# Banded attention into a gated two-layer block on one core: weights requested early, one output stage moved ahead of the second batch's attention

## The chip, the cores and the metric

The kernel runs on one core of a Trainium2 chip. The metric is device time in microseconds (us), from three runs: 324.64, 325.49 and 327.11, median 325.49. The core's engines have one instruction queue each: TensorE (PE, matmuls; its weight loads are PEld), VectorE (DVE), ScalarE (ACT), GpSimd (POOL) and SyncE (SP, which here only issues DMAs). An instruction waits for its semaphores at the head of its queue, and all behind it wait with it.

## The reference

Attention in a causal window of 128 positions with a linear bias per head (ALiBi), for 8 batches of 8 heads, 576 positions and 64 values per head; its output, as 4608 tokens by 512, goes through a two-layer block whose gate is h·sigmoid(beta·h).

```python
scores = scale * np.matmul(q, k.transpose(0, 1, 3, 2))
...
bias = slopes[:, None, None] * (-np.abs(rel).astype(np.float32))[None, :, :]
mask = (rel >= 0) & (rel < window)      # window = 128
scores = np.where(mask, scores + bias[None], -1000000000.0)
scores = scores - np.max(scores, axis=-1, keepdims=True)
attn = np.exp(scores)
attn = attn / (np.sum(attn, axis=-1, keepdims=True) + 1e-09)
return np.matmul(attn, v).astype(np.float32)
...
h = x @ w_in                      # x: (4608, 512), w_in: (512, 2048)
g = h * (1.0 / (1.0 + np.exp(-beta * h)))
return (g @ w_out).astype(np.float32)
```

## The kernel before

**Tiling.** The two-layer block works on nine groups g of 512 tokens. H(g) is 16 steps j: four matmuls of 128x512 (L557) make a 128x512 block of h in one PSUM bank, ACT takes its tanh into `sig` (L564), DVE makes (sig + 1)·h into `gT` (L565), which frees the bank. (h·sigmoid is written with tanh, a factor 0.5 comes at the end.) O(g, i, n), for four row blocks i and four parts n, is four matmuls (L588) that add gT times a quarter of w_out into one bank; after part 3 ACT copies the bank out (L598). A *chunk* below is four such matmuls, of H or of O. Weights W1 (four chunks of columns) and W2 (four chunks of rows) are requested by POOL, cast to bf16 on the way.

**Attention.** Rows of q, k, v are requested by SP (L207, L218), at most 14 staging tiles at once, cast to bf16 by POOL. For batches 0 and 1, a head pair p is transposed on PE (`TP`, L287; copied to SBUF by DVE and ACT), and visited twice: visit A has its scores in the two-bank PSUM tile SS, visit B in the two-bank tile SX (`SP_`). ACT takes the exponential; `PVP` multiplies by v and DVE normalises; `XP` transposes the result into XT, which H reads. The bias and the mask come in one of two ways: a matmul with a table (`slope` times `relb`, L324) that adds them to the scores, or a DVE multiplication of the exponentials by exp(bias) (`factor`, from the table `fallq`). The last 64 positions of a batch go their own way (TT, SCT, PV, X). From batch 2 on, DMA transposes take the place of PE ones, scores are `SC`, in SS and in ST, and `PVB` multiplies by v. H(1) needs the tail of batch 0 and the first 448 positions of batch 1.

**Order.** PE, SP and POOL run in the order that the kernel is written in; for batch 0 that holds for ACT and DVE too, after it their order is a scheduler's. The list `steps` sets what PE does between batch 0 and H(1): the H chunks of group 0 with the attention of batch 1 between them. `spread` then runs H(1), O(0) and O(1, 0 to 2), and lays the attention of batch 2 between the items from number `first` on. `b2` holds the requests, casts and DMA transposes of batch 2, one popped with each item.

**PSUM.** Eight banks: SS (2), `hps` (2), transposes (2, later ST), SX (2, later the banks `ops` and `h3`). H blocks take turns: in group 0 steps j = 0 and 3 lie in the halves of SX, the rest in `hps`; in group 1 odd steps below `FOUR[1]` lie in `h3` and `ops`.

Of the kernel before, what the change touches and what calls it, by code (L numbers as in the profile page):

```python
# [10 lines left out]
ALU = mybir.AluOpType  # L11
# [4 lines left out]
P = 128  # L16
# [3 lines left out]
def kernel(  # L20
# [142 lines left out]
    def falls_late(i):  # L163
        to, a, w = ((0, 0, P), (128, 0, 64), (192, 0, P), (320, 1, 64), (384, 1, P))[i]
        after(nc.vector.tensor_copy(
            out=falls[:, :, to : to + w], in_=fall[:, :, a, 0:w]), gates[1, 4])

    def factor(pt, m, p):

        if m:  # L170
            nc.vector.tensor_tensor(  # L171
                out=pt[:], in0=pt[:], in1=falls[:, 2 * p : 2 * p + 2], op=ALU.mult)
            return
        t = (fallq if m is None else fall)[:, 2 * p]
# [138 lines left out]
    def SP_(b, vis, p):  # L313
        qk = QK[b % 2]
        sps = SX if vis == "B" else SS
        w = WIDTH[vis]
        biased = vis == "A" or p > 1
        if biased:
            rhs = relb[:]
            if vis == "B":  # L320
                rhs = bass.AP(tensor=rhs.tensor, offset=rhs.offset,
                              ap=[list(rhs.ap[0]), [2 * P, 2], [0, 2], [1, P]])
            for e in range(2):
                nc.tensor.matmul(  # L324
                    sps[:, e, 0:w], lhsT=slope[:, 2 * p + e], rhs=rhs, start=True, stop=False,
                    skip_group_check=True)
# [13 lines left out]
        pt = pt_pool.tile([P, 2, 512], BF16, name="pt", tag="pt")  # L340
        pts[b, vis, p] = pt
        nc.scalar.activation(out=pt[:, :, 0:w], in_=sps[:, :, 0:w], func=ACTF.Exp, scale=qscale)
        if vis == "B" and b and not biased:
            factor(pt, None, p)

    def room(b, shape):

# [61 lines left out]
    def DT(b, sb):  # L409
        rows = ROWS[sb]  # L410
        src = staged.pop((b, sb))
        moved.add((b, sb))
        r = nc.sync.dma_start(
            out=QK[b % 2][:, :, :, P * sb : P * sb + rows].rearrange("d i p s -> d (i p) s"),
            in_=src[0:rows].rearrange("r i h d -> r (i h d)"), transpose=True,
        )
        if (b, sb) == (2, 0):
            after(r, w2[3])

    COLS = {0: (0, 384), 1: (128, 256), 2: (0, 384), 3: (192, 320), 4: (128, None)}  # L420

# [115 lines left out]


    gts, hs = {}, {}
    FOUR = {1: 10, 2: 8}  # L540

    def Hm(g, j, cs):
        if j == 0 and cs[0] == 0:
            gts[g] = gt_pool.tile([P, NFF, TOKG], BF16, name="gT", tag="gT")
        c0 = (g * TOKG) % XTR
        if cs[0] == 0:
            if g == 0 and j in (0, 3):
                hs[g, j] = SX[:, j // 2]
            elif j % 2 and j < FOUR.get(g, 0):
                hs[g, j] = obank("hpo", "h3" if j % 4 == 1 else "ops")  # L550
            elif g > 1 and j % 3 == 2 and j >= FOUR.get(g, 0):
                hs[g, j] = obank("hpo", "h3")
            else:
                hs[g, j] = psum_h.tile([P, TOKG], F32, name="hps", tag="hps")[:]
        hps = hs[g, j]
        for c in cs:
            nc.tensor.matmul(  # L557
                hps, lhsT=W1[:, c, bass.ts(j, P)], rhs=XT[:, c, c0 : c0 + TOKG],
                start=(c == 0), stop=(c == NDM - 1),
            )  # L560
        if cs[-1] < NDM - 1:
            return
        sig = sig_pool.tile([P, TOKG], BF16, name="sig", tag="sig")
        gates[g, j] = nc.scalar.activation(out=sig[:], in_=hps, func=ACTF.Tanh, scale=beta_h[:, j : j + 1])  # L564
        gates["gT"] = nc.vector.scalar_tensor_tensor(  # L565
            out=gts[g][:, j, :], in0=sig[:], scalar=1.0, in1=hps, op0=ALU.add, op1=ALU.mult
        )
# [6 lines left out]
    def OS(g, i, n):  # L574
        gT = gts[g]
        if n == 0:
            if g < 2:
                late[g, i] = obank("ops", "h3" if i % 2 and (g, i) != (1, 3) else "ops")
            elif i == 0 or i == 2 and g == NTG - 1:
                late[g, i] = psum_h.tile([P, DM], F32, name="oph", tag="hps")[:]  # L580
            else:
                late[g, i] = obank("ops", "ops")
# [89 lines left out]
    with tc.manual_schedule(engines={ENG.PE, ENG.SP, ENG.Pool}):  # L672
        with tc.manual_schedule(engines={ENG.Activation, ENG.DVE}):
# [22 lines left out]
            SP_(0, "A", 1)  # L696
            cast_v(0, 0)
            cast_pair(0, 2)
            w1.append(load_w1(0))
            TP(0, 2)  # L700
            M(0)
            SP_(0, "B", 1)
            cast_v(0, 1)
            idle(2)
            SP_(0, "A", 2)
            PVP(0, "A", 0)
# [4 lines left out]
            PVP(0, "A", 1)  # L711
            cast_v(0, 2)
            cast_v(0, 3)
            w1.append(load_w1(1))
            padding()
            PVP(0, "A", 2)
            SP_(0, "A", 3)
# [41 lines left out]
            cast_qk(b, 4)  # L759
            cast_v(b, 4)  # L760

        for w in ("p0", "p1", "v0", "v1", "p2", "p3", "v2", "v3"):
            n = int(w[1])
            if w[0] == "p":
                get_pair(1, n)
            else:
                get("v", 1, n)
        tail(0)
        tail(1)
        w1.append(load_w1(2))  # L770
        cast_pair(1, 0)
        cast_pair(1, 1)
        cast_v(1, 0)
        cast_v(1, 1)
        cast_pair(1, 2)
        cast_pair(1, 3)
        w1.append(load_w1(3))
        cast_v(1, 2)
        cast_v(1, 3)
        w2 += [load_w2(n) for n in range(2)]  # L780
        tail_casts(0)
        w2 += [load_w2(n) for n in range(2, 4)]
        tail_casts(1)
        OG = lambda g, i: [lambda n=n: OS(g, i, n) for n in range(4)]
        HG = lambda g: [lambda j=j: HS(g, j) for j in range(NFF)]
# [14 lines left out]
                    at += att[done][2]  # L800
                    done += 1

        b2 = blocks(2)

        def wrap(it):
            def f():
                if b2:
# [16 lines left out]
        half = lambda c: lambda: Hm(0, 15, range(c, c + 2))  # L824
        def open_s():
            trans.close()
            psum_s = ctx.enter_context(
                tc.tile_pool(name="psum_s", bufs=1, space=bass.MemoryType.PSUM))
            spans.append(psum_s.tile([P, 2, 512], F32, name="ST"))

        steps = [h[2], R(0), h[3], h[4], A(0), R(1), B_(0), h[5], A(1), h[6], R(2), B_(1), VA(0), falls_tail,
                 h[7], A(2), R(3), h[8], VA(1), B_(2), VB(0), h[9], A(3), VB(1), VA(2), h[10],
                 B_(3), open_o, lambda: TT(0), h[11], VA(3), XO(0), lambda: SCT(0), h[12], VB(2),
                 XO(1), h[13], lambda: PV(0, 4, 0), VB(3), lambda: PV(0, 4, 1), XO(2), h[14],
                 half(0), XO(3), lambda: X(0, 4), half(2)]
        for f in steps:
# [4 lines left out]
        rest = {0: [lambda: TT(1)], 2: [lambda: SCT(1)],  # L841
                4: [lambda: PV(1, 4, 0), lambda: PV(1, 4, 1)], 5: [lambda: X(1, 4), open_s]}
        items = h[:10]
        for n in range(6):
            items += [h[10 + n], o[n]] + rest.get(n, [])
        items += o[6:]
        for n in range(5):
            items.insert(18 + n, lambda n=n: falls_late(n))
# [46 lines left out]
```

The softmax here doesn't subtract the row's maximum and nothing guards it: scores larger than these inputs give would overflow.

## Time and profile before

| | |
|---|---|
| times of three runs | 324.64, 325.49, 327.11 us |
| profiled execution: span, first to last instruction | 324.0 us |
| its own time | not listed apart; the median of the runs is 1.5 us above the span |
| PE busy | 312.7 us, 97% |
| ACT, DVE, POOL busy | 60%, 57%, 30% |
| PE clock granted | full in all 40 slices, mean 0.999 |
| H(0) chunk j = 2, H(1) first chunk, H(2) first chunk on PE | start at 22.35, 49.01 and 94.23 us |

A busy PE counts the tail of each pipelined matmul, so back-to-back chunks are better read from their starts. Views that list idle time name what ended it. DMA packets of several queues share the same 16 engines.

### The profile page before, as it was taken

What the parts mean: (1) busy time and instruction counts of PE and PEld (TensorE: products, weight loads), DVE (VectorE), ACT (ScalarE), POOL (GpSimd) and SP (SyncE); (2) the same over time, 40 slices, a digit from 0 to 9 for tenths busy, and PEclk for the clock granted to TensorE, in tenths of its full rate; (3) what the DMA queues carried; (4) which work ended last, traced back from release to release, by engine and by line L of the source; (5) the groups of instructions that cost most, each with busy time, mean ns of one, the idle gap of its engine ahead of it and who ended that gap; (6) DMA issues with size and microseconds to landing.
All of it is one profiled execution on the core that took longest, in us unless ns stands there. A gap on an engine that the chain in (4) does not pass through costs nothing.

```text
span 324.0 us, 5988 instructions
## 1 busy us (share of the span) xinstructions
PE 312.7 (97%) x2297; PEld 153.3 (47%) x2297; DVE 183.1 (57%) x346; ACT 194.1 (60%) x283; POOL 98.8 (30%) x154
## 2 busy tenths in 40 slices
PE   8888999999999999999999999999999999999995
PEld 3454554443545454544454545444544455444443
DVE  5777877542548753785178717752775176335500
ACT  6857887635558865685467635845675465346511
POOL 4864820333873455356226232340000000000000
PEclk9999999999999999999999999999999999999999
DMA  7999999998999999999969994993222112110021
GB/s 221 252 263 238 176 196 196 215 199 162 214 181 208 222 208 139 230 217 148 257 153 196 150 245 94 211 138 107 18 65 60 65 18 65 46 62 32 10 90 65
DMA packets 147565, 48.84 MB, mean 151 GB/s; under 512 B 135360, under 2 KB 143824, under 8 KB 147536
## 3 DMA queue, kind: packets, MB, share of 16 engines
q1 hardware_dynamic: 115712, 32.39, 56.1%
q0 software_dynamic: 28624, 10.29, 26.1%
q10 hardware_dynamic: 3200, 5.78, 5.1%
q8 instruction: 18, 0.29, 0.4%
q14 instruction: 11, 0.09, 0.1%
HBM read 36.71 MB, written 9.44 MB: 142 GB/s over the span
## 4 chain that ended last, share of the span: by engine, by line
PE 69%; DMA 17%; SPq 6%; POOL 2%; ACT 2%; DVE 2%; issue 1%; POOLq 0%; DVEq 0%
PE ops L588 21%; PE hps L557 21%; PE hpo L557 10%; PE oph L588 7%; DMA fst<-in_v_dram 6%; DMA qkT<-bst 6%; SPq L207 3%; DMA fst<-in_q_dram 3%; DMA fst<-in_k_dram 2%; PE SS L438 2%; SPq L218 2%; PE ST L438 1%; PE SS L495 1%; PE SS L492 1%; POOL bst L229 1%
## 5 line engine op out<-in xcount | busy, mean ns | idle before, releaser
L588 PE MATMUL ops<-W,gT 128*128 128x512 bf16 (+1 forms) x464 | 109.7, 372 | 0.5 <-ACT osb L598 0.5
L565 DVE SCALAR_TENSOR_TENSOR gT<-sig,hps 128x512 bf16<-128x512 bf16 x100 | 67.6, 683 | 71.8 <-ACT sig L564 71.5
L557 PE MATMUL hps<-XT,W 128*128 128x512 bf16 x400 | 99.9, 379 | 0.3 <-DVE XT L533 0.3
L564 ACT ACTIVATE sig<-hps,beta_h 128x512 bf16<-128x512 f32 x100 | 68.1, 690 | 34.6 <-PE hps L557 33.2
L588 PEld LDWEIGHTS <-gT 128*128 128x128 bf16 x592 | 55.7, 98 | 61.6 <-issue 1.9
L557 PEld LDWEIGHTS <-W 128*128 128x128 bf16 x576 | 52.9, 98 | 60.8 <-issue 3.6
L228 POOL CAST bst<-fst 128x512 bf16<-128x512 f32 (+1 forms) x32 | 20.8, 650 | 74.4 <-DMA fst<-in_q_dram 42.4
L557 PE MATMUL hpo<-XT,W 128*128 128x512 bf16 x168 | 43.1, 379 | 0.0
L564 ACT ACTIVATE sig<-hpo,beta_h 128x512 bf16<-128x512 f32 x42 | 29.0, 690 | 16.9 <-PE hpo L557 16.9
L565 DVE SCALAR_TENSOR_TENSOR gT<-sig,hpo 128x512 bf16<-128x512 bf16 x42 | 28.6, 681 | 11.2 <-ACT sig L564 11.0
L598 ACT ACTIVATE osb<-ops 128x512 f32<-128x512 f32 (+1 forms) x28 | 16.6, 595 | 25.5 <-PE ops L588 25.5
L446 ACT ACTIVATE pt<-SS 128x1024 bf16<-128x1024 f32 x24 | 24.5, 1020 | 11.6 <-PE SS L438 11.1
L588 PE MATMUL oph<-W,gT 128*128 128x512 bf16 x128 | 29.3, 379 | 0.0
L229 POOL CAST bst<-fst 128x512 bf16<-128x512 f32 (+1 forms) x32 | 22.1, 690 | 15.6 <-DMA fst<-in_k_dram 15.0
L176 DVE TENSOR_TENSOR pt<-pt,fall 128x1024 bf16<-128x1024 bf16 x24 | 17.1, 712 | 14.8 <-ACT pt L446 14.8
L446 ACT ACTIVATE pt<-ST 128x1024 bf16<-128x1024 f32 x24 | 24.5, 1022 | 0.0
L171 DVE TENSOR_TENSOR pt<-pt,falls 128x1024 bf16<-128x1024 bf16 x24 | 18.8, 791 | 9.3 <-ACT pt L446 9.3
L250 POOL DMA_DIRECT2D vs<-in_v_dram x25 | 21.3, 869 | 0.2 <-issue 0.2
L598 ACT ACTIVATE osb<-oph 128x512 f32<-128x512 f32 x8 | 4.8, 597 | 21.1 <-PE oph L588 21.1
L495 PEld LDWEIGHTS <-pt 128*128 128x128 bf16 x240 | 14.8, 97 | 4.2
L243 POOL CAST vs<-fst 128x512 bf16<-128x512 f32 (+1 forms) x15 | 10.5, 703 | 15.9 <-DMA fst<-in_v_dram 15.9
L438 PEld LDWEIGHTS <-qkT 64*128 64x128 bf16 x240 | 8.9, 94 | 12.5 <-issue 12.0
(102 smaller groups left out, 257.8 us busy)
## 6 DMA issues: line engine op xcount, KB each, us to landing
fst<-in_k_dram SPq DMA_DIRECT2D x32, 256.0 KB, 6.0
fst<-in_q_dram SPq DMA_DIRECT2D x32, 256.0 KB, 5.3
out_dram<-osb ACTq DMA_DIRECT2D x22, 256.0 KB, 2.0
fst<-in_v_dram SPq DMA_DIRECT2D x12, 256.0 KB, 5.4
out_dram<-osb POOLq DMA_DIRECT2D x12, 256.0 KB, 5.2
vs<-in_v_dram POOLq DMA_DIRECT2D x20, 128.0 KB, 6.1
W<-in_moe_w_in_dram POOLq DMA_DIRECT2D x4, 512.0 KB, 7.9
W<-in_moe_w_out_dram POOLq DMA_DIRECT2D x4, 512.0 KB, 12.8
```

The lines of the kernel that those rows point to most:

```text
L171: nc.vector.tensor_tensor(out=pt[:], in0=pt[:], in1=falls[:, 2 * p : 2 * p + 2], op=ALU.mult)
L228: nc.gpsimd.tensor_copy(out=t[0:rows, 0], in_=fs.pop(("q", b, sb))[0:rows])
L229: return nc.gpsimd.tensor_copy(out=t[0:rows, 1], in_=fs.pop(("k", b, sb))[0:rows])
L250: return nc.gpsimd.dma_start(out=VS[b % 2][0:rows, sb, :, 0:D], in_=v[b, :, P * sb : P * sb + rows, :].rearrange("h p d -> p h d"))
L438: nc.tensor.matmul(o, lhsT=qk[64 * e : 64 * e + 64, 1, p, P * kb : P * kb + P], rhs=qk[64 * e : 64 * e + 64, 0, p, P * kb : P * kb + nq], ...
L446: nc.scalar.activation(out=pt[:], in_=sps[:], func=ACTF.Exp, scale=qscale)
L495: nc.tensor.matmul(o, lhsT=weights(b, qb, h, 0), rhs=vs[:, qb, h, 0 : D + 1], start=qb == 0, stop=True, skip_group_check=True)
L557: nc.tensor.matmul(hps, lhsT=W1[:, c, bass.ts(j, P)], rhs=XT[:, c, c0 : c0 + TOKG], start=(c == 0), stop=(c == NDM - 1),)
L564: gates[g, j] = nc.scalar.activation(out=sig[:], in_=hps, func=ACTF.Tanh, scale=beta_h[:, j : j + 1])
L565: gates["gT"] = nc.vector.scalar_tensor_tensor(out=gts[g][:, j, :], in0=sig[:], scalar=1.0, in1=hps, op0=ALU.add, op1=ALU.mult)
L588: nc.tensor.matmul(ops_[:, cols], lhsT=gT[:, j, i * P : i * P + P], rhs=W2[:, j, cols], start=(j == 0), stop=(j == NFF - 1),)
L598: nc.scalar.mul(o, ops_[:, cols], 0.5)
```

## The change

Both weight matrices are requested from POOL at the start (W1's first chunk after one more cast, the other seven right behind batch 0's casts). Group 0 runs all of H(0), then parts 0 to 2 of O(0, 0 to 2), and only then the attention of batch 1 with the remaining seven O chunks between its steps. The first request for batch 1's rows waits until the third chunk of W2 has landed. Batch 1 uses no bias matmuls: every exponential is multiplied on DVE, visit A by two new multiplications. H(0) has its even steps in SX, in turns of the two halves; O(0) uses `hps` and one half of SX. In the following stage O(0) is gone, all odd steps of H(1) lie in `h3` and `ops`, and batch 2's attention begins at item 16 in place of 36.

```diff
     def falls_late(i):
...
-            out=falls[:, :, to : to + w], in_=fall[:, :, a, 0:w]), gates[1, 4])
+            out=falls[:, :, to : to + w], in_=fall[:, :, a, 0:w]), gates[0, 15])
     def factor(pt, m, p):
+        if m == "A":
+            t = fallq[:, 2 * p]
+            x = pt[:, :, 0:256].rearrange("k e (n q) -> k e n q", n=2)
+            nc.vector.tensor_tensor(
+                out=x, in0=x, in1=bass.AP(tensor=t.tensor, offset=t.offset,
+                                          ap=[list(t.ap[0]), [2 * P, 2], [0, 2], [1, P]]), op=ALU.mult)
+            nc.vector.tensor_tensor(
+                out=pt[:, :, 256:384], in0=pt[:, :, 256:384], in1=fallq[:, 2 * p : 2 * p + 2, 1],
+                op=ALU.mult)
+            return
...
-        biased = vis == "A" or p > 1
+        biased = b == 0 and (vis == "A" or p > 1)
...
-        if vis == "B" and b and not biased:
-            factor(pt, None, p)
+        if b:
+            factor(pt, None if vis == "B" else "A", p)
...
-        if (b, sb) == (2, 0):
-            after(r, w2[3])
...
-    FOUR = {1: 10, 2: 8}
+    FOUR = {1: 16, 2: 8}
...
-            if g == 0 and j in (0, 3):
-                hs[g, j] = SX[:, j // 2]
+            if g == 0 and j % 2 == 0:
+                hs[g, j] = SX[:, j // 2 % 2]
...
-            if g < 2:
+            if g == 0:
+                late[g, i] = (SX[:, 0] if i == 2 else
+                              psum_h.tile([P, DM], F32, name="oph", tag="hps")[:])
+            elif g < 2:
                 late[g, i] = obank("ops", "h3" if i % 2 and (g, i) != (1, 3) else "ops")
...
-            w1.append(load_w1(0))
             TP(0, 2)
             M(0)
             SP_(0, "B", 1)
             cast_v(0, 1)
+            w1.append(load_w1(0))
...
-            w1.append(load_w1(1))
+            w1 += [load_w1(n) for n in range(1, 4)]
+            w2 += [load_w2(n) for n in range(4)]
...
-        for w in ("p0", "p1", "v0", "v1", "p2", "p3", "v2", "v3"):
...
+        first = None
+        for w in ("p0", "p1", "v0", "p2", "v1", "p3", "t", "v2", "v3"):
...
+                r = get_pair(1, n) if w[0] == "p" else get("v", 1, n)
+                if first is None:
+                    first = r
+                    after(r, w2[2])
...
-        steps = [h[2], R(0), h[3], h[4], A(0), R(1), B_(0), h[5], A(1), h[6], R(2), B_(1), VA(0), falls_tail,
-                 h[7], A(2), R(3), h[8], VA(1), B_(2), VB(0), h[9], A(3), VB(1), VA(2), h[10],
-                 B_(3), open_o, lambda: TT(0), h[11], VA(3), XO(0), lambda: SCT(0), h[12], VB(2),
-                 XO(1), h[13], lambda: PV(0, 4, 0), VB(3), lambda: PV(0, 4, 1), XO(2), h[14],
-                 half(0), XO(3), lambda: X(0, 4), half(2)]
+        o = [OG(0, i) for i in range(4)]
+        steps = h[2:] + [falls_tail] + [o[i][n] for n in range(3) for i in range(3)]
+        steps += [lambda n=n: falls_late(n) for n in range(5)]
+        steps += [o[0][3], R(0), o[1][3], A(0), R(1), o[2][3], B_(0), A(1), R(2), o[3][0], B_(1), VA(0), A(2), R(3),
+                  o[3][1], VA(1), B_(2), VB(0), A(3), o[3][2], VB(1), VA(2), B_(3), open_o,
+                  lambda: TT(0), o[3][3], VA(3), XO(0), lambda: SCT(0), VB(2), XO(1),
+                  lambda: PV(0, 4, 0), VB(3), lambda: PV(0, 4, 1), XO(2), XO(3), lambda: X(0, 4)]
...
-        h, o = HG(1), two(0) + OG(0, 2) + OG(0, 3) + two(1)
-        o += OG(1, 2)
-        items = h[:10]
-        for n in range(6):
-            items += [h[10 + n], o[n]] + rest.get(n, [])
-        spread([wrap(it) for it in items], 36, len(items) - 2, need[2])
+        h, o = HG(1), two(1) + OG(1, 2)
+        items = h[:8] + [lambda: TT(1), h[8], lambda: SCT(1), h[9], h[10], lambda: PV(1, 4, 0),
+                         lambda: PV(1, 4, 1), h[11], lambda: X(1, 4), open_s] + h[12:] + o
+        spread([wrap(it) for it in items], 16, len(items) - 2, need[2])
```

Here `two(g)` is O(g, 0) and O(g, 1) in turns; R, A, B_, VA, VB and XO are batch 1's TP, visits A and B of `SP_`, `PVP` of each, and `XP`.

More of the change, by code (lines that the diff above doesn't have):

```diff
@@ L760, in tail_casts @@
             cast_v(b, 4)
-        for w in ("p0", "p1", "v0", "v1", "p2", "p3", "v2", "v3"):
-            n = int(w[1])
-            if w[0] == "p":
-                get_pair(1, n)
-            else:
-                get("v", 1, n)
-        tail(0)
+        first = None
+        for w in ("p0", "p1", "v0", "p2", "v1", "p3", "t", "v2", "v3"):
+            if w == "t":
+                tail(0)
+            else:
+                n = int(w[1])
+                r = get_pair(1, n) if w[0] == "p" else get("v", 1, n)
+                if first is None:
+                    first = r
+                    after(r, w2[2])
+        b2 = blocks(2)
+        b2.pop(0)()
         tail(1)
-        w1.append(load_w1(2))
         cast_pair(1, 0)
@@ L773 @@
         cast_v(1, 0)
+        cast_pair(1, 2)
         cast_v(1, 1)
-        cast_pair(1, 2)
         cast_pair(1, 3)
-        w1.append(load_w1(3))
+        tail_casts(0)
         cast_v(1, 2)
         cast_v(1, 3)
-        w2 += [load_w2(n) for n in range(2)]
-        tail_casts(0)
-        w2 += [load_w2(n) for n in range(2, 4)]
         tail_casts(1)
@@ L801, in spread @@
                     done += 1
-        b2 = blocks(2)
         def wrap(it):
@@ L822, in open_o @@
                 tc.tile_pool(name="psum_o", bufs=1, space=bass.MemoryType.PSUM))
-        half = lambda c: lambda: Hm(0, 15, range(c, c + 2))
         def open_s():
@@ L838 @@
         done = 0
-        h, o = HG(1), two(0) + OG(0, 2) + OG(0, 3) + two(1)
-        o += OG(1, 2)
-        rest = {0: [lambda: TT(1)], 2: [lambda: SCT(1)],
-                4: [lambda: PV(1, 4, 0), lambda: PV(1, 4, 1)], 5: [lambda: X(1, 4), open_s]}
-        items = h[:10]
-        for n in range(6):
-            items += [h[10 + n], o[n]] + rest.get(n, [])
-        items += o[6:]
-        for n in range(5):
-            items.insert(18 + n, lambda n=n: falls_late(n))
-        spread([wrap(it) for it in items], 36, len(items) - 2, need[2])
+        h, o = HG(1), two(1) + OG(1, 2)
+        items = h[:8] + [lambda: TT(1), h[8], lambda: SCT(1), h[9], h[10], lambda: PV(1, 4, 0),
+                         lambda: PV(1, 4, 1), h[11], lambda: X(1, 4), open_s] + h[12:] + o
+        spread([wrap(it) for it in items], 16, len(items) - 2, need[2])
         for g in range(2, NTG):
```

## The prediction

> **What bounds the kernel now.** I read the page's busy times first, then the chain, then TensorE's own timeline with the idle time in brackets. The page says that PE is the bound from end to end, at full clock:
>
> ```profile
> PE 312.7 (97%) x2297; PEld 153.3 (47%) x2297; DVE 183.1 (57%) x346; ACT 194.1 (60%) x283; POOL 98.8 (30%) x154
> ...
> PEclk9999999999999999999999999999999999999999
> ```
>
> The chain at the start of H(1) shows the price of a chunk (four matmuls) when nothing holds PE: from 50.03 to 56.08 seven chunks start 0.863 apart. Four banks take turns there (two `hps`, two `hpo`).
>
> ```profile
> 50.03 0.86 PE hpo L557 x4
> 50.90 0.86 PE hps L557 x4
> 51.76 0.86 PE hpo L557 x4
> ```
>
> So what counts is PE work plus the moments in which PE stands. In the wait view of PE these are small: the longest between 5 and 300 us is 0.7. From H(0)'s chunk j = 2 (22.35) to the first of H(1) (49.01) PE has 26.65 us, of which 23.8 are work (added up from the chain's pieces) and 2.8 are waits; from there to H(2) (94.23) 45.2, with 0.5 of waits. The change rearranges just these two stretches; I price each, against the profiled execution's span of 324.0. The median of the runs, 325.49, is 1.5 more, and I add that at the end.
>
> **H(0) in one piece: the banks.** This is the largest term, and one line of the timeline carries it (start, duration, engine, line, what; the idle time in brackets):
>
> ```profile
> 23.48 0.68 DVE L565 SCALAR_TENSOR_TENSOR gT<-sig,SX 128x512 bf16<-128x512 bf16 x1
> ...
> 24.21 1.02 PE L557 MATMUL SX<-XT,W 128*128 128x512 bf16 x4 [0.39 <-DVE gT L565]
> 25.07 1.03 PE L557 MATMUL hps<-XT,W 128*128 128x512 bf16 x4
> ...
> 25.27 0.69 ACT L564 ACTIVATE sig<-SX,beta_h 128x512 bf16<-128x512 f32 x1 [0.61 <-PE SX L557]
> ...
> 25.99 0.69 DVE L565 SCALAR_TENSOR_TENSOR gT<-sig,SX 128x512 bf16<-128x512 bf16 x1
> ```
>
> The chunk at 24.21 is j = 3, in the second half of SX. It waited for the DVE operation that ended at 24.16, which reads j = 0 out of the *first* half. SX is one tile, and its two halves are not told apart. In the changed kernel's instruction order all eight even chunks of H(0) write SX, and each waits for the DVE multiplication of the even chunk before. By these rows a chunk frees SX 2.52 us after its start: 0.86 on PE, 0.20 to ACT's start, 0.69 tanh, 0.03, 0.69 on DVE, 0.05 back. In that time PE does two chunks, 1.72, so it stands 0.8 per pair. j = 2 must wait until 24.21 as j = 3 did before. Then j = 14 starts at 24.21 + 6 × 2.52 = 39.33, and H(0) ends at 41.05; free of waits it would be 22.35 + 14 × 0.863 = 34.4. Cost: 6.6.
>
> **O(0), parts 0 to 2.** Nine chunks, 7.8. The second needs the `hps` bank of j = 15, free 1.66 after H(0)'s end; one chunk covers 0.86, so 0.8 is lost. PE reaches the rest at 49.6.
>
> **Batch 1's attention with seven O chunks.** PE work, from rows of before: 7 chunks 6.0; transposes 4 × 0.54; scores A 4 × 0.27, B 4 × 0.33; P·v 4 × 0.31 and 4 × 0.33; XP 4 × 0.22; tail (TT, SCT, PV, X) 1.3. Sum 15.3. The bias matmuls are gone, by the chain 0.33 four times and 0.43 twice: 2.2 saved. In their place come DVE multiplications. Those of visit A (512 and 256 elements) are not in the trace; copies of 1024 and 512 take 0.42 and 0.28, a multiplication of 1024 0.69. Between those bounds, 0.4 and 1.1 for the pair, I take 0.6, since they are smaller than the 1024 ones; they run beside PE, and moving them over these ends moves the end from -0.2 to +0.8.
>
> What PE waits for, walking each engine's queue in the built order with these durations: 0.9 before B(0), whose SX still holds the third O block (its ACT copy is 0.6); 0.8 before TT, for a transpose bank; 1.8 before PV, because SCT → exponential → multiplication is
>
> ```profile
> 42.71 1.06 ACT L400 ACTIVATE pc<-SS 128x1024 bf16<-128x1024 f32 x1
> ...
> 43.80 0.80 DVE L403 TENSOR_TENSOR pc<-pc,fallt 128x1024 bf16<-128x1024 bf16 x1 [0.71 <-ACT pc L400]
> ```
>
> and only 0.5 of PE work is left to lay over it, where before there were H chunks; 1.4 at the end (normalise, XP, X, copies to XT); 0.3 in small ones. Sum 5.2. H(1) then starts at 49.6 + 15.3 + 5.2 = 70.1. Before it started at 49.0, with O(0)'s 16 chunks (13.8) still to do, so the like point is 62.8: **+7.3**.
>
> **H(1) and batch 2's first scores.** Before, batch 2's scores lay between O chunks that ask nothing of ACT; now they lie among H(1)'s last four. Four places: SCT 0.2, PV 0.4 and X 0.9 (two or one chunk lie over each of these chains, where four lay before), and then O(1, 0). That block takes the bank `ops` straight behind j = 15, which used it. ACT's order is: two exponentials of scores (0.91 apart when adjacent, as in the rows 74.99 and 75.91 of ACT's timeline), then the tanh of j = 15. ACT is 0.5 behind by then because the pair of exponentials before delayed three tanhs. From the end of these scores: exponentials start at 0.7, tanh at 2.6 to 3.3, DVE multiplies the second exponential to 3.4, then j = 15's product to 4.0. PE finished j = 15 at 0.9: a wait of 3.1. Further 0.5 in small ones. Sum 5.2 instead of 0.5: **+4.7**. One gain: batch 3's transposed rows come earlier against PE, so the wait of 0.5 for them behind the first two H(2) chunks goes: **-0.5**. Behind that PE is bound by its own work as before.
>
> **Weights and rows.** While W2 flowed, at 46 to 48 us, the two DMA queues moved (packets, MB, share of the 16 engines; q0 holds POOL's requests, q1 SP's)
>
> ```profile
> q0 software_dynamic: 319, 0.31, 91.9%
> q1 hardware_dynamic: 318, 0.08, 30.1%
> ```
>
> In 2 us that is 319 packets of 1 KB, and a chunk has 512: 3.2 us each while sharing, 2.95 at a full share; 3.5 by the poorest such slice (290 packets, at 44 to 46). Seven requests from 14.9 on, 0.74 of POOL each, keep behind them only memsets and casts of rows that aren't there yet. First landing at most 6.7 later (the shortest landing of before), then 3.2 apart: W1 complete by 28.0, W2's third chunk at 37.6, the last at 40.8. They are wanted at 36.8, 47.0 and 49.6. Batch 1's first request waits on SP for 37.6, with all later requests behind it; its rows land from 41 to 44 on and are cast by 45, wanted at 50.5. The 3.5 MB up to the last v tile take 15 us at 230 GB/s (the page's slices show 196 to 263): 54, wanted at 59.7. So memory is hidden, by some 5 us; at 3.5 a chunk it still is. That cover comes from the slow H(0): without it the rows would be late by up to 3.
>
> **Sum.** 324.0 + 7.3 + 4.7 - 0.5 = 335.5, with 1.5 around it **337.0**.
>
> The longest new wait is 3.1 us; no row of before has such a gap between 5 and 300 us, and the clock is full throughout. The Trainium skill (TensorE: Matmul & The Clock Gate, Part 1: The HAM clock gate) speaks against leaving PE idle: an idle window of about 3.4 us puts the clock to half. By the trace the price is nothing, by the page an estimate of 1.7 us more for one window, if the gap fills it; no run here shows it.
>
> **Rivals.**
> - *Not slower: banks come free in time.* If a bank held PE no longer than the next chunk lasts (0.86 instead of 1.66 after its matmuls), H(0) loses nothing (-6.6), O(0) nothing (-0.8), and O(1, 0) nothing (-3.1): 326.5, within 1%. For it: the seven chunks at 0.863 above, on four banks. Against: the wait at 24.21, on two halves of one tile. It decides from a release under 0.9. 0.05.
> - *Half of it.* The wait at H(0) comes as told, the ACT backlog at O(1, 0) and the tail of batch 1 don't, because the queues run closer than my walk: 328.8 to 332. 0.06.
> - *Rows late after all.* If POOL's queue alone needed 5 us a chunk, W2's third would land near 47 and batch 1 would start some 4 late: 341 to 345. Against: 3.2 while sharing. 0.05.
> - *The change doesn't put the attention "inside" O(0).* It doesn't much: nine of 16 chunks run ahead of it. That is in the forecast.
>
> **How the numbers follow.** The forecast, 337.0, has 0.82, with 332 to 341: H(0)'s term is known within 1, the two walks within 1.5 each, and the ends of the DVE pairs. A measurement of this kernel, with runs 0.8% apart, tells about 1% (3.3 us) from no change. Slower by more than that (the forecast, half of it, late rows): 0.93; within: 0.05; faster: 0.02, for which all the waits and more would have to go: the bias matmuls and every wait of the first stretch are 5.0 together.
>
> **What would show it.** In the profile after: SX chunks of H(0) with idle time ended by DVE's `gT`, some 0.8 each and 6.6 in all; H(0) ending near 41; H(1) starting near 70; the first `ops` chunk of O(1, 0) idle for some 3 us, ended by DVE's `gT`; H(2) near 106; the bias matmuls (L324, then L334) at 12 in place of 24. Even chunks 1.72 apart would refute the largest term; waits of PE for DMA in this stretch would mean the rival of late rows.

## The result, and the profile after

The changed kernel takes 342.28 us (four executions, 340.55 to 343.88), the kernel before 325.06 beside it: 1.0519 times as long, 95% interval 1.0463 to 1.0576 (the ratio as recorded; the two medians alone give 1.0530). The forecast was 337.0, with 332 to 341: the side was right, the size 5.3 us short, outside that range. The profiled execution is the shortest of the four, 340.55 us with a span of 338.8, against 324.0 before.

The page of the changed kernel, busy time of PE and the clock granted to it in 40 slices of 8.5 us:

```profile
PE 312.0 (92%) x2244; PEld 153.1 (45%) x2285; DVE 189.1 (56%) x356; ACT 194.7 (57%) x283; POOL 100.5 (30%) x154
...
PEclk9998999999979999999999999999999999999999
```

PE is busy as long as before (312.7) in a span 14.8 longer, so it stands. New, and not in the forecast's sum: two slices are not at full clock. The first surprise to look into is therefore the clock, the second where PE stands. The view of PE's waits between 18 and 115 us names the places. Each line gives who waited, for whom, us in total, times, and the longest:

```profile
PE SX L565 <- DVE gT L573: 5.1, 6, 1.9
PE ops L599 <- DVE gT L573: 2.6, 1, 2.6
PE pv L480 <- DVE pc L413: 1.7, 2, 1.5
PE tpt L311 <- DVE xnp L369: 1.4, 1, 1.4
PE tps L297 <- DVE xnp L369: 0.7, 1, 0.7
PE oph L599 <- DVE gT L573: 0.7, 1, 0.7
PE SX L345 <- ACT osb L609: 0.7, 1, 0.7
...
```

The first line is H(0): its even chunks in the two halves of SX. The second is O(1, 0) behind step 15 of H(1). The other lines shown lie in batch 1's attention, except the 0.7 on `oph`, O(0)'s second chunk, and 0.2 on `pv`. No line of the whole view names DMA. PE's timeline shows what the waits do at H(0) and at O(1, 0):

```profile
24.72 1.53 PE L565 MATMUL SX<-XT,W 128*128 128x512 bf16 x4 [1.92 <-DVE gT L573]
26.04 1.91 PE L565 MATMUL hps<-XT,W 128*128 128x512 bf16 x4
27.75 1.41 PE L565 MATMUL SX<-XT,W 128*128 128x512 bf16 x4
29.00 1.03 PE L565 MATMUL hps<-XT,W 128*128 128x512 bf16 x4
30.66 1.02 PE L565 MATMUL SX<-XT,W 128*128 128x512 bf16 x4 [0.63 <-DVE gT L573]
...
93.38 3.55 PE L599 MATMUL ops<-W,gT 128*128 128x512 bf16 x8 [2.58 <-DVE gT L573]
```

From 30.66 on, SX chunks follow each other every 2.51 to 2.53 us, as forecast. But the first two pairs took 3.03 and 2.91, and the eight matmuls (two chunks) at 93.38 took 3.48 up to the next work, where two chunks take 1.73 elsewhere. The view by windows (length, busy PE and its instructions, granted clock, DMA share, GB/s) says why:

```profile
24.00:25.00 1.00, 0.28 (x2) 1.00 1.22 204
25.00:26.00 1.00, 1.00 (x4) 0.55 1.21 158
27.00:28.00 1.00, 1.00 (x4) 0.50 1.26 208
28.00:29.00 1.00, 1.00 (x5) 0.74 1.21 187
29.00:30.00 1.00, 1.00 (x5) 1.00 1.24 200
...
92.00:93.00 1.00, 0.00 (x0) 1.00 1.34 235
93.00:94.00 1.00, 0.62 (x2) 0.68 1.12 180
95.00:96.00 1.00, 1.00 (x4) 0.50 1.09 202
96.00:97.00 1.00, 1.00 (x7) 0.61 0.61 125
97.00:98.00 1.00, 1.00 (x15) 1.00 0.81 184
```

Twice PE ran at half clock for about 3.4 us (added up over these windows and the ones between), each time right behind a rest of PE: 1.9 and 2.6 us in the timeline above.

The table sets this against the forecast by stages. H(0) goes from its first matmul to O(0)'s first; then comes O(0) with batch 1's attention, to H(1); then H(1)'s stage, to H(2); then the rest, to the end. All stages are differences of starts in PE's timeline, in us; the span begins some 19 to 20 us before H(0). The last column is the mean clock of that execution:

| kernel | H(0) | O(0), attention | H(1) stage | rest | span | clock |
|---|---|---|---|---|---|---|
| forecast (21.6 = 41.05 - 19.44; 29.05 = 70.1 - 41.05; 36.1 = 45.2 - 13.8 + 4.7) | 21.6 | 29.05 | 36.1 | 229.3 | 335.5 | full |
| changed kernel | 22.5 | 29.7 | 37.2 | 229.4 | 338.8 | 0.990 |
| H(0) in other banks | 15.0 | 29.2 | 37.1 | 229.4 | 330.7 | 0.995 |
| O(1, 0) in another bank | 21.6 | 28.8 | 32.8 | 229.4 | 332.4 | 0.999 |
| two rests filled | 21.8 | 30.0 | 37.2 | 229.5 | 337.8 | 0.993 |
| four rests filled | 21.8 | 30.2 | 35.8 | 229.4 | 336.2 | 1.000 |
| 16 O chunks in the attention | 21.6 | 23.7 | 36.9 | 229.4 | 331.2 | 0.995 |
| both banks, W1 as before | 15.0 | 29.2 | 35.1 | 229.4 | 328.1 | 0.998 |
| all of it, rows earlier | 15.2 | 31.7 | 33.0 | 229.3 | 328.4 | 0.990 |

(Before: first matmul to H(1) 29.6, H(1) to H(2) 45.2, rest 229.8.) The lower rows are experiments that follow; the number in brackets at each experiment is its run's.

### The profile page after: what moved, and what is told of

Read it like the earlier page. It is cut to its first block, busy times and chain, and to the rows that moved or that the text cites. A ratio compares the mean times of both kernels' runs of the same rounds, so it can differ in the third digit from the quotient of the medians.

```text
span 338.8 us, 5934 instructions
## 1 busy us (share of the span) xinstructions
PE 312.0 (92%) x2244; PEld 153.1 (45%) x2285; DVE 189.1 (56%) x356; ACT 194.7 (57%) x283; POOL 100.5 (30%) x154
## 4 chain that ended last, share of the span: by engine, by line
PE 78%; DVE 8%; ACT 5%; DMA 3%; SPq 2%; issue 2%; POOL 1%; DVEq 0%; ACTq 0%
PE ops L599 24%; PE hps L565 20%; PE oph L599 10%; PE hpo L565 9%; DVE gT L573 3%; PE SX L565 2%; ACT sig L572 2%; DMA fst<-in_v_dram 2%; PE SS L446 2%; PE ST L446 1%; PE SS L503 1%; DMA qkT<-bst 1%; ACT pt L454 1%; PE SS L500 1%; SPq L228 1%
## 5 line engine op out<-in xcount | busy, mean ns | idle before, releaser
L573 DVE SCALAR_TENSOR_TENSOR gT<-sig,hps 128x512 bf16<-128x512 bf16 x91 | 61.5, 683 | 70.2 <-ACT sig L572 69.9
L599 PE MATMUL ops<-W,gT 128*128 128x512 bf16 (+1 forms) x384 | 94.1, 375 | 4.1 <-DVE gT L573 2.6
L565 PE MATMUL hps<-XT,W 128*128 128x512 bf16 x353 | 89.7, 382 | 1.0 <-DVE XT L541 0.4
L572 ACT ACTIVATE sig<-hps,beta_h 128x512 bf16<-128x512 f32 x91 | 61.9, 689 | 32.0 <-PE hps L565 28.8
L565 PE MATMUL hpo<-XT,W 128*128 128x512 bf16 x174 | 45.6, 379 | 0.4 <-issue 0.2
L599 PE MATMUL oph<-W,gT 128*128 128x512 bf16 x171 | 40.5, 379 | 1.1 <-DVE gT L573 0.7
L572 ACT ACTIVATE sig<-hpo,beta_h 128x512 bf16<-128x512 f32 x45 | 31.1, 690 | 18.0 <-PE hpo L565 15.3
L609 ACT ACTIVATE osb<-ops 128x512 f32<-128x512 f32 (+1 forms) x24 | 14.1, 593 | 23.8 <-PE ops L599 23.6
L503 PEld LDWEIGHTS <-pt 128*128 128x128 bf16 x240 | 14.7, 97 | 4.5 <-ACT pt L454 0.4
L245 POOL CAST bst<-fst 128x512 bf16<-128x512 f32 x16 | 10.3, 650 | 21.5 <-PE hps L565 14.2
L500 PEld LDWEIGHTS <-pt 128*128 128x128 bf16 x192 | 13.4, 97 | 2.8
```

The costliest lines, as they stand in the source:

```text
L503: nc.tensor.matmul(o, lhsT=weights(b, qb, h, 0), rhs=vs[:, qb, h, 0 : D + 1], start=qb == 0, stop=True, skip_group_check=True)
L565: nc.tensor.matmul(hps, lhsT=W1[:, c, bass.ts(j, P)], rhs=XT[:, c, c0 : c0 + TOKG], start=(c == 0), stop=(c == NDM - 1),)
L573: gates["gT"] = nc.vector.scalar_tensor_tensor(out=gts[g][:, j, :], in0=sig[:], scalar=1.0, in1=hps, op0=ALU.add, op1=ALU.mult)
L599: nc.tensor.matmul(ops_[:, cols], lhsT=gT[:, j, i * P : i * P + P], rhs=W2[:, j, cols], start=(j == 0), stop=(j == NFF - 1),)
L609: nc.scalar.mul(o, ops_[:, cols], 0.5)
```

## The experiments

**Is it the banks? (1)** Theory: PE stands because a PSUM tile is released late, and the long rests cost clock on top. Rival: the weights' packets, or PSUM traffic, slow the chunks. The edit gives H(0)'s even steps the two transposition banks in place of SX's halves.

```diff
-            if g == 0 and j % 2 == 0:
-                hs[g, j] = SX[:, j // 2 % 2]
+            if g == 0 and j == 0:
+                hs[g, j] = SX[:, 0]
+            elif g == 0 and j % 2 == 0:
+                hs[g, j] = psum_t.tile([P, TOKG], F32, name="hpt", tag="t")[:]
```

> The changed kernel, with the even steps of H(0) from j = 2 on in the two transposition banks, which stand empty there, instead of in the halves of SX. Bank theory: PE stood because SX is released as one tile, and the two half-speed stretches of 3.4 us came from the gaps. Then the six SX waits (1.9 and five of 0.63) are gone, chunks follow each other every 0.863, the half-speed stretch of 24.7 to 29 is gone too, j = 2 starts near 22.9 and H(0) ends near 35.0 in place of 42.5: 7.5 us less, of which late rows of batch 1 may take 0 to 2 back (its last pair was cast by 48.4): 332.5 to 336 against 342.3. Rival, the half speed is the weights' packets or PSUM traffic and not the gap: the chunks at 24 to 29 stay about 1.5 apart, H(0) ends near 37. Rival, late rows: PE waits for casts at the first transposes of batch 1 and the gain stays under 4. The wait and the half speed at O(1, 0) stay, since nothing is changed there.

Measured: 333.11 us, 1.0219 [1.0184, 1.0254]. PE's timeline of this kernel:

```profile
22.94 1.02 PE L567 MATMUL hpt<-XT,W 128*128 128x512 bf16 x4
23.80 1.03 PE L567 MATMUL hps<-XT,W 128*128 128x512 bf16 x4
24.66 1.03 PE L567 MATMUL hpt<-XT,W 128*128 128x512 bf16 x4
```

Chunks follow every 0.863, O(0) begins at 35.02: H(0) is 7.5 shorter, as expected, at full clock. The same weight packets flow beside it, so they are not what slowed it. No wait for batch 1's rows appears (0.6 for a transposed row of batch 2, later). At O(1, 0), untouched, wait and half clock stay (2.48, and 3.54 for the eight matmuls).

**The second bank (2).** Does the slow stretch at 93 us come from the rest ahead of it?

```diff
+            elif g == 1 and i == 0:
+                late[g, i] = psum_h.tile([P, DM], F32, name="oph", tag="hps")[:]
             elif g < 2:
                 late[g, i] = obank("ops", "h3" if i % 2 and (g, i) != (1, 3) else "ops")
```

> The changed kernel, with O(1, 0) in an hps bank instead of ops, so that it does not wait for the product of j = 15. Bank theory: the wait of 2.6 goes, and with it the half-speed stretch behind it, 1.75: about 4.3 less, 338.0 against 342.3. Rival, the half speed at 93 to 97 comes from what runs then (scores, exponentials) and not from the gap: 2.6 less only, 339.7, and the eight O chunks still take near 3.5. Rival, the wait only moves to O(1, 1) in h3: under 1 less. H(0) is as in the changed kernel.

Measured: 336.69 us, 1.0321 [1.0278, 1.0364]. PE's timeline at that place:

```profile
87.79 1.04 PE L565 MATMUL hpo<-XT,W 128*128 128x512 bf16 x4
88.66 1.03 PE L601 MATMUL oph<-W,gT 128*128 128x512 bf16 x4
89.53 1.03 PE L601 MATMUL ops<-W,gT 128*128 128x512 bf16 x4
```

The H(1) stage falls by 4.4, from 37.23 to 32.83: wait and half clock both gone, as expected; the median is 1.3 under the expected 338.0. The profiled execution held something more: the same wait of 1.92 at H(0) as in the changed kernel, and *no* half clock behind it.

```profile
24.00:26.00 2.00, 1.45 (x7) 1.00 1.14 181
```

So a rest of 1.9 may cost clock or not. The four executions had mean clocks of 0.999, 0.995, 0.994 and 0.990, and took 334.17, 336.39, 336.99 and 338.31: here the times scatter with the number of half-clock stretches that an execution happens to get.

**Fill the rests, keep the waits (3).** Dummy matmuls, whose results nobody reads, lie in two waits; the banks stay as they are.

```diff
-        steps = h[2:] + [falls_tail] + [o[i][n] for n in range(3) for i in range(3)]
+        steps = [lambda: idle(8)] + h[2:] + [falls_tail] + [o[i][n] for n in range(3) for i in range(3)]
...
         h, o = HG(1), two(1) + OG(1, 2)
+        o[0] = lambda f=o[0]: (calm(12), f())
```

> The changed kernel, with two stretches of dummy matmuls whose results nobody reads: 8 ahead of H(0)'s j = 2 (1.7 us, inside the wait of 1.9) and 12 ahead of O(1, 0) (2.6 us, inside the wait of 2.6). The waits for the banks stay; only PE no longer rests. If the half speed comes from PE resting: j = 2 still starts near 24.7, but the first two pairs take 2.52 each instead of 3.03 and 2.91 (0.9 less), and the eight matmuls of O(1, 0) take 1.73 instead of 3.48 (1.75 less): 2.6 less together, 339.7 against 342.3. If it comes from memory traffic, PSUM traffic or from the kind of matmul: no gain, 342.3, or up to 1 more where the dummies run past the waits at half speed.

Measured: 340.05 us, 1.0411 [1.0361, 1.0461]. Both places ran at full clock: pairs of 2.52 from the start, and 1.89 for the eight matmuls (3.55 in the same column before). Against that, a half-clock stretch came in a place that I had not filled, at the end of batch 1's attention. PE had stood 1.4 and 1.5 us there, with 2.7 us of work between them; the stretch begins some 2 us after the second rest:

```profile
67.00:68.00 1.00, 0.00 (x0) 1.00 1.04 224
...
70.00:71.00 1.00, 0.60 (x6) 0.74 1.18 242
71.00:72.00 1.00, 0.69 (x2) 0.50 1.16 212
72.00:73.00 1.00, 1.00 (x3) 0.50 2.22 140
73.00:74.00 1.00, 1.00 (x4) 0.55 0.34 63
```

The median met the expectation, by way of another place than I had in mind.

**Fill four rests (5).** Six dummies each ahead of TT and of PV as well.

```diff
-                  lambda: TT(0), o[3][3], VA(3), XO(0), lambda: SCT(0), VB(2), XO(1),
-                  lambda: PV(0, 4, 0), VB(3), lambda: PV(0, 4, 1), XO(2), XO(3), lambda: X(0, 4)]
+                  lambda: more(6), lambda: TT(0), o[3][3], VA(3), XO(0), lambda: SCT(0), VB(2), XO(1),
+                  lambda: more(6), lambda: PV(0, 4, 0), VB(3), lambda: PV(0, 4, 1), XO(2), XO(3), lambda: X(0, 4)]
```

> The changed kernel with dummy matmuls in its four long waits of PE (8 and 12 as in the run before with two, and 6 each ahead of batch 1's tail: ahead of TT, wait 1.4, and ahead of PV, wait 1.5). With two of them filled, three of four executions still had a mean clock of 0.993 to 0.995, one 0.999 with 336.99 us, and the profiled one was at half speed at 70.7 to 73.5, right behind the two waits not filled. If the half speed follows stretches in which PE rests, whether or not any single rest is long, then all executions have 0.998 or more now, and all take what the waits and the work alone make: 336.5 to 338, against 342.3 (and the forecast of 337.0). If it follows something else, for instance DMA traffic, executions with 0.990 to 0.995 stay and the median stays near 340.

Measured: 338.93 us, 1.041 [1.035, 1.047]. The page of this kernel has the clock full in all slices:

```profile
PEclk9999999999999999999999999999999999999999
```

Mean clocks 1.000, 1.000, 0.999 and once 0.995; times 338.54, 337.93, 339.33 and 341.81. The changed kernel had 0.990 three times and 0.985. So PE's rests are what costs most of the clock; nothing else was taken away. One execution in four still had a stretch, against my expectation, and the median is 0.9 above the expected range: O(0) and attention took 30.2, so the dummies were in the way by 0.5 to 1.4. Against the changed kernel the ratio falls from 1.052 to 1.041, 3.5 us, the price of the clock (more, if the dummies' own cost is added). As the two intervals just overlap, it is known within some 3 only; that the clock costs time at all is seen in the profiles, at the two places.

**Batch 1 without bias matmuls, alone (4).** Put into the kernel before, with the new branch of `factor` as in the change:

```diff
...
-        biased = vis == "A" or p > 1
+        biased = b == 0 and (vis == "A" or p > 1)
...
-        if vis == "B" and b and not biased:
-            factor(pt, None, p)
+        if b:
+            factor(pt, None if vis == "B" else "A", p)
```

> The kernel before, with one part of the change alone: no bias matmuls in batch 1 (12 fewer, 2.2 us of PE), each of its exponentials multiplied on DVE instead, visit A by two operations (0.74 and 0.2 to 0.6 in the changed kernel). In the stretch from j = 2 to H(1) DVE was busy for 21.0 of 26.7 us and PE for 24.6; this adds some 5.2 to DVE and takes 2.2 from PE, so DVE becomes the bound with 26.2. Theory: the matmuls' gain is given back by DVE, -1 to +1.5: 324 to 326.5 against 325.1. Rival, the multiplications hide: 322.9, faster by 0.7%. Rival, DVE's queue delays the tanh products and the banks of H(0): over 327.

Measured: 326.42 us, 1.0004 [0.9975, 1.0033]: no difference. From 22.35 to 49.01 the kernel before (first line) and this kernel (second) have:

```profile
22.35:49.01 26.66, 24.58 (x257) 12.88 (x256) 21.00 (x47) 22.14 (x34) 12.96 (x20) 1.00 1.10 203
22.35:49.01 26.66, 22.54 (x241) 12.10 (x245) 25.28 (x58) 21.92 (x34) 13.20 (x19) 1.00 1.16 208
```

(The busy times are PE's, weight loads', DVE's, ACT's, POOL's.) PE lost 2.0 of work and DVE gained 4.3, to 95% of the stretch. PE's waits that DVE ended rose from 1.2 to 2.9 between 20 and 60 us (added up from the views of waits). So the saving was real and DVE took it back.

**Cover for the attention (6).** All 16 O(0) chunks between the attention's steps, none ahead but the first; the O blocks all in `hps`.

```diff
-                late[g, i] = (SX[:, 0] if i == 2 else
-                              psum_h.tile([P, DM], F32, name="oph", tag="hps")[:])
+                late[g, i] = psum_h.tile([P, DM], F32, name="oph", tag="hps")[:]
...
+        c = [o[i][n] for i in range(4) for n in range(4)]
...
+        steps = h[2:] + [falls_tail, c[0], R(0), c[1], c[2], A(0), R(1), B_(0), c[3], A(1), c[4], R(2), B_(1), VA(0),
+                         c[5], A(2), R(3), c[6], VA(1), B_(2), VB(0), c[7], A(3), VB(1), VA(2), c[8], B_(3), open_o,
...
```

> The changed kernel with all 16 O(0) chunks laid between the steps of batch 1's attention, one block after the other in the two hps banks, in place of nine ahead of it and seven inside. Theory: the waits of that attention (5.8 of 21.1) and the one ahead of O(0)'s second chunk (0.7) are missing cover: with two chunks over each chain instead of one or none they fall to about 1.5, H(1) starts near 67.2 in place of 72.2, and of the half-speed stretches the ones in this part go: 342.3 - 5 = 337.3, from 336 to 338.5. Rival, DVE is the bound there (its multiplications, normalisations and copies), cover or not: H(1) starts at 69.5 or later, a gain under 2.7. Rival, the rows of batch 1, now wanted 8 earlier, are late: PE's first transposes wait for POOL's casts. H(0) and O(1, 0) are not touched.

Measured: 332.65 us, 1.020 [1.015, 1.025], better than expected. From 38 to 66 us these are all the waits of PE, and the first still belongs to H(0):

```profile
PE SX L565 <- DVE gT L573: 0.6, 1, 0.6
PE pv L384 <- ACT qkT L303: 0.3, 1, 0.3
PE pv L384 <- POOL vs L253: 0.2, 1, 0.2
```

The stage takes 23.7 where its work is 23.1 (16 chunks 13.8, attention 9.3): 6.0 less than in the changed kernel. DVE's and ACT's chains were as long as ever; what they lacked was PE work to lie beside. The rows, wanted 8 to 10 us earlier, still came in time. The mean clock was 1.000 in two executions and 0.995 in two: with fewer rests, fewer half-clock stretches.

**Put together (7, 8).** Both banks mended and W1's first request back ahead of the `v` cast; then also 16 chunks in the attention, with batch 1's rows behind W1's last chunk, since they are wanted earlier.

```diff
+            w1.append(load_w1(0))
             TP(0, 2)
...
             cast_v(0, 1)
-            w1.append(load_w1(0))
...
-                    after(r, w2[2])
+                    after(r, w1[3])
```

> The changed kernel with three things mended: H(0)'s even steps in the transposition banks, O(1, 0) in an hps bank, and W1's first request back at its place of the kernel before. If the terms add: the run with the first (332.5 in its profile, which had one half-speed stretch at O(1, 0)) less 2.5 for the wait and 1.75 for the clock there, less 0.5 at the start, which would be seen as H(0)'s second step starting near 22.4 in place of 22.9: 327.7, up to 329.5 where an execution still has one half-speed stretch behind batch 1's tail. What is left over the kernel before (326.3 in those comparisons) is then the attention without H chunks over it. Rival, the terms overlap (the ACT backlog at O(1, 1) takes the place of the one at O(1, 0)): 330 or more.

> The changed kernel with the three things of the run beside it, all 16 O(0) chunks between the attention's steps, and batch 1's rows requested behind W1's last chunk in place of W2's third, as they are wanted 8 us earlier. By PE work alone: from the second H(0) step at 22.4, 14 H chunks 12.1, 16 O chunks 13.8 and attention 9.3 make H(1) start at 57.6; with 2 to 4 of waits 59.6 to 61.6, where the kernel before has 62.8 at the like point; its H(1) stage costs up to 1.2 more than there. So 323 to 327 against 326.3: it may just beat both kernels. Rival, DVE is the bound between H(0) and H(1): 327 to 329. Rival, rows or W2's last chunks late because they now share the DMA queues: PE waits for POOL or DMA, over 329.

Measured: 330.27 us, 1.0133 [1.0073, 1.0193], and 330.63, 1.014 [1.0096, 1.0184]. Both miss. The terms do not add, because something new stands in the way. PE's waits in the first, from 30 to 100 us, and in the second, from 30 to 60:

```profile
PE SS L446 <- DMA qkT<-bst: 2.4, 2, 1.5
...
PE tps L297 <- POOL vs L253: 0.9, 1, 0.9
```

```profile
PE tps L297 <- POOL bst L245: 2.9, 2, 1.6
PE pv L384 <- POOL vs L253: 1.6, 2, 0.8
```

In the first it is above all batch 2's transposed rows, now wanted 8.5 us sooner; in the second the casts of batch 1's rows, which wait for their DMA. The half clock came back behind these rests too (mean clock 0.990 in the second's profile).

**Can the loading be arranged better? (9, 10, 12)** The last kernel with five, then with eight O chunks ahead of the attention, then with eight and the rows behind W2's third chunk again. The lists differ as in

```diff
-        steps = h[2:] + [falls_tail, c[0], R(0), c[1], c[2], A(0), R(1), B_(0), c[3], A(1), c[4], R(2), B_(1), VA(0),
+        steps = h[2:] + [falls_tail] + c[:5] + [R(0), c[5], A(0), R(1), B_(0), A(1), c[6], R(2), B_(1), VA(0),
...
```

> The run with everything mended, but with five O(0) chunks ahead of batch 1's first transposes in place of one, and eleven between the attention's steps. Theory: that run lost 4.8 to rows that came late (POOL's casts, which wait for DMA) and some 3.5 to half-speed stretches at 42 to 45 and 52 to 56 behind those rests. 3.5 us of work ahead covers most of the lateness; the rests then stay under 1 and so does the loss of clock: from O(0) to H(1) 24 to 26 in place of 31.7, time 323 to 326 against 325.4 of the kernel before: no difference or a little faster. Rival, eleven chunks are too thin a cover: DVE's and ACT's chains come back as waits, 27 or more, and time over 326.

> The same with eight O(0) chunks ahead and eight between. If lateness of the rows is what is left, this gains as much as the run with five ahead or up to 1 more; if cover is what is left, it loses 1.5 to 3 against it, since its attention then has about as little over it as in the changed kernel (seven chunks, waits of 5.8, some of them from the third O block lying in SX, which is not so here). Expected by the theory: 325 to 328.

> The run with eight O(0) chunks ahead and eight between, but with batch 1's rows requested behind W2's third chunk again, as in the changed kernel. In the runs with five and eight ahead PE stood 4.7 and 3.9 for W2's chunks, which shared the queues with the rows. Theory: alone on the queues W2 is in time (so it was in the run with the first bank mended), the rows, cast from 38 to 48, are just in time behind eight chunks, and O(0) to H(1) falls from 32.1 to about 25.5; but batch 2's rows, requested last, now come late against H(1)'s stage (2.4 of waits for the transposed rows with nine chunks ahead, up to 4 more here), so that half or more of it is given back: 326 to 329.5, still not under the kernel before. Rival, memory is not the limit of this stretch: no wait for DMA appears at batch 2's scores, and the time is 323 to 325.

Measured: 330.64 us, 1.0137 [1.0106, 1.0169]; 330.62, 1.0145 [1.0102, 1.0188]; 330.01, 1.0128 [1.0104, 1.0152]. All three miss. Waits of PE in the three, from 34 to 48, 34 to 66 and 30 to 64 us:

```profile
PE oph L602 <- DMA W<-in_moe_w_out_dram: 4.7, 2, 2.9
```

```profile
PE oph L602 <- DMA W<-in_moe_w_out_dram: 3.9, 2, 2.9
```

```profile
PE pv L384 <- POOL vs L253: 2.2, 2, 1.3
PE SS L345 <- ACT qkT L303: 1.2, 2, 0.7
```

Rows ahead of W2: the weights are late. Weights ahead of the rows: the rows are late. Five arrangements end between 1.0128 and 1.0145, standing at four different transfers, most with a half-clock stretch behind the rest. That points to a common limit, the bytes that are wanted before 65 us. It isn't proven: I tried no kernel with fewer bytes, and the 2.2 in the last one comes from `v` tiles that the changed kernel requests behind three tail tiles, an order I left alone. A rival is left as well, the staging tiles: in runs 8 and 9 SP stood 8.3 and 9.0 us at one request for batch 1's rows until a cast of POOL had ended.

**Early weights alone (11).** In the kernel before, all weight requests in one row at 15 us.

```diff
-            w1.append(load_w1(1))
+            w1 += [load_w1(n) for n in range(1, 4)]
+            w2 += [load_w2(n) for n in range(4)]
...
-        w1.append(load_w1(2))
...
-        w1.append(load_w1(3))
...
-        w2 += [load_w2(n) for n in range(2)]
...
-        w2 += [load_w2(n) for n in range(2, 4)]
```

> The kernel before with the early weight requests alone: W1's second to fourth chunk and all of W2 requested by POOL in one row at 15 us, without any wait of batch 1's rows for them; order, banks and tables as before. There batch 1's attention lies inside H(0) and wants its rows from 23 to 35 us. Theory: the weights take most of the DMA queues until 40 (2.5 to 3.2 us a chunk), rows get a third of them, so the later pairs and v tiles, cast at 28 to 35 before, come 5 to 15 later, and PE waits for POOL's casts: 331 to 341. That would show why early weights ask for H(0) and O(0) to come ahead of the attention. Rival, sharing hardly hurts the rows: under 328.

Measured: 339.19 us, 1.0399 [1.0356, 1.0442]. PE's waits, 22 to 60 us:

```profile
PE tps L287 <- POOL bst L235: 8.6, 3, 6.9
PE pv L374 <- POOL vs L243: 1.3, 2, 0.8
```

As expected: batch 1's third pair comes late, PE stands 6.9 at one place, and runs at half clock for some 10 us around it. So early weights don't go with the order of before. The order with H(0) and O(0) ahead of the attention wants the rows later, and pays for it with the banks and the cover that the change took away.

## Why the prediction was short

- **H(0) in SX, 6.6: right.** The mechanism was named, the wait is there in six chunks, and at full clock the stage takes 21.6 (O(1, 0) in another bank), the forecast's 21.6. In other banks it takes 15.0.
- **O(0)'s second chunk, 0.8: right** (0.70).
- **Batch 1's attention, 15.3 of work and 5.2 of waits: right, a little small.** 28.8 to 29.7 with O(0)'s first part, forecast 29.05. The pair of multiplications of visit A, put at 0.6 between 0.4 and 1.1, took 0.69 to 1.43: the 128x256 one 0.28 or 0.69, the 128x512 one 0.42 to 0.83 (the last section has what goes with it). That may be the 1.4 ahead of TT where I had 0.8; no run changed it alone. All such excesses come to 0.7 in the profiled execution and to nothing in that of the kernel with O(1, 0) in another bank. Part of the agreement is luck: the three named waits, put at 0.9, 0.8 and 1.8, took 0.7, 1.4 and 1.5, so that their errors cancel.
- **H(1) stage, +4.7: right but for the clock.** The wait at O(1, 0) was 2.76 from the end of step 15, forecast 3.1; without it the stage takes 32.8, forecast 33.0 (36.1 - 3.1). (The terms of that stage's sum add up to 5.1, not 5.2.) Behind H(2) 0.4 was gained, forecast 0.5.
- **The step that failed: "By the trace the price is nothing".** The effect of the new waits on the clock entered the sum as 0, because the trace of before has no such gap. It measures 0.9 at H(0) and 1.75 at O(1, 0) in the profiled execution, some 3.5 in the medians (against the kernel with four rests filled). The absence of a row is not a row: the sum had to take in the price of half clock behind *each* new rest, and the range at least its size. The Trainium skill (TensorE: Matmul & The Clock Gate, Part 1: The HAM clock gate) speaks of about 3.4 us for both the window and the stay; here the stay agrees (3.4), but rests of 1.9 and 2.6 were enough, so its length of rest doesn't hold in this case. The page also says that the window runs freely, which would fit a rest of 1.9 that costs once and not the next time; no run here shows the window itself.
- **What is left:** 0.5 at the start (19.94 for 19.44), which need not be the change's: H(0)'s first matmul lies between 19.05 and 20.03 in the profiles of six kernels that all begin in the same way. With 0.25 between execution and span, the sum of the profiled one closes, with H(0), the attention, H(1)'s stage and the start in this order: 337.0 + 0.9 + 0.7 + 1.1 + 0.5 + 0.25 = 340.5. The median is 1.7 above it. The clock explains that in part only: the slowest execution (343.88) has the lowest mean clock, 0.985, but two with the 0.990 of the profiled one took 0.9 and 2.6 longer. The kernel before, run beside the experiments, took 324.62 to 328.23 at mean clocks of 0.998 to 1.000, so a scatter of that size is there at full clock too; its cause stays open.
- **Memory hidden, "without it the rows would be late by up to 3": half right.** PE waits for no DMA in the changed kernel up to 115 us, and batch 1's first request left at 34.2, forecast 37.6. With H(0) mended alone no row of batch 1 was late; with H(0) and the cover mended PE stands at rows or weights that come late.
- **The bias matmuls: as counted,** 12 in place of 24. The lines of the changed kernel's page by group:

```profile
L334 PE MATMUL SS<-relb,slope 128*128 128x384 bf16 x8 | 2.0, 327 | 0.1
L334 PE MATMUL SX<-relb,slope 128*128 128x512 bf16 x4 | 1.2, 380 | 0.0
```

The rivals fell: banks were not free in time, ACT's backlog came as told, rows were not late. None of the kernels run beats the one before; the nearest, with the tables alone (4), equals it. Of the three causes, each mended alone gives back 3.0% (banks), 2.0% (O(1, 0)) and 3.2% (cover) of the 5.2%, clock included; together they stop at 1.3%.

## What to carry to other kernels

Count the time until a PSUM tile is free again (matmuls, ACT, DVE: 2.5 us here) against the PE work that may run meanwhile; the halves of one tile are one tile. Work that is moved out of a chain of ACT and DVE operations takes its cover with it: price the chain bare. And price every rest of PE of some 2 us, or several shorter ones close together, twice: once as the wait and once, with a chance, as up to 1.7 us of half clock behind it (half of the 3.4 us measured here).

## What the runs showed of the hardware that I had not expected

- TensorE drops to half clock for about 3.4 us behind rests as short as 1.9 us, or behind two shorter ones close together (1.4 and 1.5 us in the run with two rests filled, 1.3 and 0.9 us just ahead of 53.4 us in run 12); the same rest costs in one profile and not in another. Dummy matmuls in four rests brought the mean clock from 0.985 to 0.990 up to 0.995 to 1.000. The kernel before is not quite free of it: two of its 45 executions beside the experiments had a mean clock of 0.995, and they are its slowest (329.49 and 329.38 us).
- The same DVE multiplication of 128x256 took 0.28 in some calls and 0.69 in others within one execution. The timelines of DVE and POOL in the changed kernel have a slow call inside a cast of POOL, and a fast one with no cast beside it:

```profile
58.88 0.28 DVE L176 TENSOR_TENSOR pt<-pt,fallq 128x256 bf16<-128x256 bf16 x1
64.08 0.69 DVE L176 TENSOR_TENSOR pt<-pt,fallq 128x256 bf16<-128x256 bf16 x1
...
63.83 0.80 POOL L239 CAST bst<-fst 128x512 bf16<-128x512 f32 x1
```

In the profiles of the twelve kernels with this multiplication all 20 slow calls began while a cast of POOL ran, and 27 of the 28 fast ones did not. So POOL's casts go with it; no run takes the casts away to show it.
